# Coarser first weight loads, row tiles made ready in parts, and the first contexts evicted by one engine, in a fused normalise, attention and feed-forward kernel

## The chip, the cores and the metric

The kernel runs on one core of one Trainium2 chip. The metric is the device time of that core in microseconds (us), one number per execution. The time is the span of the profile plus about 1.8 us (924.28 and a span of 922.5 before the change), so differences of spans are differences of times.

## The reference, cut to what matters

```python
xn = _layernorm(A_x)                       # [2048, 640], bf16
# A: attention; 32 heads of 192, keys and values: the last 512 positions
q = (xn @ wq) ... ; p = softmax(q k^T * 192**-0.5); o = p v
s = o.reshape(2048, 32 * 192) @ wo
# B: feed-forward, F = 1536
g = silu((silu(xn @ w_gate) * (xn @ w_up)) @ w_down)
return A_x + s * g
```

The first 170 us or so are normalisation and feed-forward; the rest is attention, two heads (a pair) at a time, the 2048 rows in four blocks of 512.

## The kernel before

The **first loads** and the **head**: nothing can be multiplied before a row tile (128 rows) of x is loaded, normalised, transposed into `xnT` and its first weights are there. The four row tiles of block 0 are run one after the other through three hidden groups (`wg_sb` and `wu_sb`, 128 columns each), so that TensorE can start as soon as one row tile is ready.

```python
def load_x(t, eng=nc.sync):
    x_t[t] = lnx.tile([P, D], bf, name="x_t")
    if t == 0:
        for r, eng in ((lo, nc.sync), (hi, nc.scalar)):          # two halves, two queues
            eng.dma_start(out=x_t[t][r, :], in_=x2[t * P + r.start : t * P + r.stop, :])
    else:
        eng.dma_start(out=x_t[t][:], in_=x2[t * P : (t + 1) * P, :])
# ...
load_x(0)
load_x(1, nc.scalar)
for cs in (slice(0, 1), slice(1, 3), slice(3, NC)):              # 1, 2 and 2 of 5 chunks
    if cs.stop == NC:
        load_x(2)
    for eng, w_sb, w in ((nc.sync, wg_sb, B_w_gate), (nc.scalar, wu_sb, B_w_up)):
        src = w[cs.start * P : cs.stop * P, 0:FQ].rearrange("(c p) f -> p c f", p=P)
        eng.dma_start(out=w_sb[:, cs, 0:FQ], in_=src)
load_x(3)
# ... remaining weights, x tiles 4 to 7
nc.scalar.activation(act_t[:], one_t[:], ACT.Sqrt)               # table load
# ...
def ready(t):                       # transposes on TensorE, then a copy out of PSUM
    ln_transpose(t)
    n = NC if t else 2
    nc.scalar.copy(xnT[:, 0:n, rows], tps[t][:, 0:n, :])
    if n < NC:
        nc.vector.tensor_copy(out=xnT[:, n:NC, rows], in_=tps[t][:, n:NC, :])
# ...
for t in range(4):
    # order of the 30 matmuls of row tile t: chunk by chunk for t == 0
    for k, (f, s, cs) in enumerate(order):
        if k == len(order) * 3 // 5 and t < 3:
            ...                     # apply row tile t + 1, ready(t + 1)
        hidden_mm(first[f][s][:, rows], s, f, rows, cs)
```

The **normalisation of the next block** is spread over the hidden groups `f` of the current one, with a transposing DMA per row tile:

```python
if nx and 1 <= f < 5:
    ln_stats(4 * b + 3 + f)
    if f == 4:
        ln_rstd(b + 1, 0, 4)
if nx and 5 <= f < 9:
    ln_apply(4 * b + f - 1)
    ln_transpose_dma(4 * b + f - 1)
```

And the **attention part**: `q_rows` projects the queries in ten row-tiled matmuls and lets the held second half of an output projection in (`between`) before its last chunk; `divide` evicts a context (the product of probabilities and values) from PSUM. For the first two blocks of all, and for most of the last pair, the eviction was shared by VectorE and ScalarE:

```python
for c in range(NC):
    if c == NC - 1 and between:
        between()
    # two matmuls of chunk c
# ...
for k in range(2):
    if k == 0 and alone:            # VectorE, one instruction of 384 columns
        nc.vector.tensor_tensor(...)
        continue
    for h in range(2):              # ScalarE, two of 192 columns
        nc.scalar.activation(...)
```

The softmax here doesn't subtract the row's maximum and nothing guards it: scores larger than these inputs give would overflow.

Of the kernel before, what the change touches and what calls it, by code (L numbers as in the profile page):

```python
# [15 lines left out]
def kernel(  # L16
# [13 lines left out]
    nc = tc.nc  # L30
# [37 lines left out]
    qpool = ctx.enter_context(tc.tile_pool(name="att_q", bufs=2))  # L68
    psum = ctx.enter_context(tc.tile_pool(name="psum", bufs=2, space=bass.MemoryType.PSUM))

    def sc_tile():
        return psum.tile([P, 2, 512], f32, name="sc", tag="sc")

    def mm_tile():
        return psum.tile([P, 2, 512], f32, name="mm", tag="mm")

# [88 lines left out]
    with ExitStack() as fctx:  # L165
# [14 lines left out]
        def load_x(t, eng=nc.sync):  # L180
            x_t[t] = lnx.tile([P, D], bf, name="x_t")
            if t == 0:
                for r, eng in ((lo, nc.sync), (hi, nc.scalar)):
                    eng.dma_start(out=x_t[t][r, :], in_=x2[t * P + r.start : t * P + r.stop, :])
            else:
                eng.dma_start(out=x_t[t][:], in_=x2[t * P : (t + 1) * P, :])

# [8 lines left out]

        load_x(0)
        load_x(1, nc.scalar)
        for cs in (slice(0, 1), slice(1, 3), slice(3, NC)):
            if cs.stop == NC:  # L200
                load_x(2)
            for eng, w_sb, w in ((nc.sync, wg_sb, B_w_gate), (nc.scalar, wu_sb, B_w_up)):
                src = w[cs.start * P : cs.stop * P, 0:FQ].rearrange("(c p) f -> p c f", p=P)
                eng.dma_start(out=w_sb[:, cs, 0:FQ], in_=src)
        load_x(3)
        load_gu(1)
        for t in range(4, 8):
            load_x(t)
        load_gu(2)
        load_gu(3)  # L210
        nc.sync.dma_start(out=wd_sb[:], in_=B_w_down.rearrange("(f p) d -> p f d", p=P))


        nc.scalar.activation(act_t[:], one_t[:], ACT.Sqrt)
        warm = sc_tile()

        def keep_warm(n):
            for _ in range(n):
                nc.tensor.matmul(warm[:, 0, :], zero_t[:, 0:P], zero_t[:], start=True, stop=True)

        keep_warm(11)

# [34 lines left out]

        tps = {}

        def ln_transpose(t):  # L260
            xn = xns.pop(t)
            tps[t] = tp[:, t % 2, 0 : NC * P].rearrange("p (c k) -> p c k", c=NC)
            for c in range(NC):
                nc.tensor.transpose(tps[t][:, c, :], xn[:, c * P : (c + 1) * P], ident[:])

        def ln_transpose_dma(t):
# [18 lines left out]

        def ffn_hidden(b, f):
            gu = mm_tile() if (b, f) == (0, 3) else sc_tile()
            for s in range(2):
                hidden_mm(gu[:, s, :], s, f, slice(b * 512, (b + 1) * 512))
            hidden_gate(b, f, gu[:, 0, :], gu[:, 1, :])  # L290

# [26 lines left out]


        first = {f: [sc[:, s, :] for s in range(2)] for f, sc in ((0, sc_tile()), (1, sc_tile()))}  # L320
        tp = psum.tile([P, 2, 1024], bf, name="tp", tag="mm")
        first[2] = [mm[:, s, :] for mm in (mm_tile(),) for s in range(2)]
        def ready(t):
            ln_transpose(t)
            rows = slice(t * P, (t + 1) * P)
            n = NC if t else 2
            nc.scalar.copy(xnT[:, 0:n, rows], tps[t][:, 0:n, :])
            if n < NC:
                nc.vector.tensor_copy(out=xnT[:, n:NC, rows], in_=tps[t][:, n:NC, :])

        ln_stats(0)
        ln_sqrt(0)
        ln_stats(1, lambda: ln_apply(0, (slice(0, 2 * P), slice(2 * P, D))))
        ready(0)
        ln_sqrt(1)
        keep_warm(3)
        banks = [(f, s) for f in range(3) for s in range(2)]
        for t in range(4):
            rows = slice(t * P, (t + 1) * P)

            order = [(*fs, [c]) for c in range(NC) for fs in banks]
            if t:
                order = [(*fs, range(NC)) for fs in banks]
            for k, (f, s, cs) in enumerate(order):
                if k == len(order) * 3 // 5 and t < 3:
                    if t == 1:
                        ln_stats(3, lambda: ln_apply(2))
                    else:
                        ln_apply(t + 1)
                    ready(t + 1)  # L350
                    if t == 0:
                        ln_stats(2)
                    if t < 2:
                        ln_sqrt(t + 2)
                    else:
                        nc.scalar.activation(act_t[:], one_t[:], ACT.Silu)
                hidden_mm(first[f][s][:, rows], s, f, rows, cs)
                if t == 3 and s == 1:
                    hidden_gate(0, f, *first[f])
        nc.gpsimd.memset(V_p[:, :, :, Dh : Dh + 2], 1.0)  # L360

        for b in range(NB):
# [4 lines left out]
            for f in range(NF):  # L367
                if nx and b and f == 0:
                    for t in range(4 * b + 4, 4 * b + 8):
                        load_x(t)  # L370
                if b or f >= 3:
                    ffn_hidden(b, f)
                if nx and 1 <= f < 5:
                    ln_stats(4 * b + 3 + f)
                    if f == 4:
                        ln_rstd(b + 1, 0, 4)
                if nx and 5 <= f < 9:
                    ln_apply(4 * b + f - 1)
                    ln_transpose_dma(4 * b + f - 1)

# [40 lines left out]
    def q_rows(i, j, between=None):  # L421
# [4 lines left out]
        for c in range(NC):  # L426
            if c == NC - 1 and between:
                between()
            for h, r in enumerate((lo, hi)):
                nc.tensor.matmul(  # L430
                    q_ps[:, h, :], pairs[pr]["wq"][r, c, j * P : (j + 1) * P], xnT[r, c, b * 512 : (b + 1) * 512],
                    start=(c == 0), stop=(c == NC - 1),
                )
# [17 lines left out]
    def pv(i, q2):  # L451
# [4 lines left out]
        def part(p):  # L456
            if p == 0:
                if q2 == 0:
                    Obs[i] = opool.tile([P, 4, 2, Dh], bf, name="O_b")
                    tag = "OT_l" if late(i) and pr < last else "OT_b"  # L460
                    OTs[i] = otpool.tile([P, 12, P], bf, name=tag, tag=tag, bufs=2 if tag == "OT_l" else 3)
                st["alone"] = i < 2 or (pr == last and 2 * b + q2 < 5)
                st["acc"] = sc_tile() if st["alone"] and q2 and b < 2 else mm_tile()
            acc = st["acc"]
# [14 lines left out]
            if p == 3:  # L479
                divide(i, q2, acc, st["alone"])  # L480

        return [lambda p=p: part(p) for p in range(4)]

    def divide(i, q2, acc, alone):
        pr, b = divmod(i, NB)
# [4 lines left out]
        for k in range(2):  # L490
            qt = 2 * q2 + k
            a_k = a_v[:, k, :, :]
            if k == 0 and alone:
                nc.vector.tensor_tensor(
# [13 lines left out]
    def pv_full(i, q2):  # L508
# [6 lines left out]
        O_b, OT_b = Obs[i], OTs[i]  # L515
        alone = i < 2 or (pr == last and 2 * b + q2 < 5)
        acc = sc_tile() if alone and b == 1 else mm_tile()
        for k in range(2):
            qt = 2 * q2 + k
            for h in range(2):  # L520
                for kc in range(KC):
# [4 lines left out]
                    )  # L526
        divide(i, q2, acc, alone)

# [245 lines left out]
```

## Time and profile before

| | before |
|---|---|
| time, median of 3 runs | 924.18 us (924.05 to 924.45) |
| span of the profiled execution | 922.5 us |
| TensorE busy | 99% of the span |
| first real matmul | 6.88 us |
| row tiles 1, 2, 3 start | 9.79, 11.91, 14.02 us |
| first 512-column matmul ("end of the head") | 15.69 us |
| last group of matmuls | 918.04 us |

How to read it: with TensorE busy for 99% there are few places where time can be won: what lies before the end of the head, single stalls after it, and the tail behind the last matmul. Two distances will be used all along: the **end of the head**, where the first matmul of 512 columns starts, and the distance **from there to the last group of matmuls** (918.04 - 15.69 = 902.35 us before), which holds every stall that comes later.

### The profile page before, as it was taken

How to read it: one execution, taken by the hardware profiler on the slowest of the kernel's cores; microseconds unless marked ns; L12 is line 12 of the kernel's file. 1: busy time of each engine (PE TensorE's matmuls, PEld its weight loads, DVE VectorE, ACT ScalarE, POOL GpSimd, SP SyncE). 2: the span in 40 equal slices, each digit the busy share in tenths (PEclk: the TensorE clock that was granted, in tenths of full speed). 3: DMA queues.
4: the chain of work that ended last, by engine and by line, in shares of the span. 5: the costliest groups of instructions: out<-in, count | busy, mean ns of one | idle time of the engine just before them, and what ended most of it. 6: DMA issues, size and time to landing. Idle time of an engine off the chain costs nothing.

```text
span 922.5 us, 25778 instructions
## 1 busy us (share of the span) xinstructions
PE 915.9 (99%) x11085; PEld 624.4 (68%) x11101; DVE 575.7 (62%) x847; ACT 473.7 (51%) x847; POOL 101.6 (11%) x390
## 2 busy tenths in 40 slices
PE   9999999999999999999999999999999999999998
PEld 5455555575858586868686767676777777676666
DVE  6433331467676767676666667676767676767656
ACT  4222223556464656555556565655555555556561
POOL 0000000000000000000000000000000000002978
PEclk9999999999999999999999999999999999999999
DMA  9321510044544434444536262525271817163534
GB/s 293 78 53 35 114 35 1 1 74 93 88 78 83 83 79 88 72 93 65 102 57 109 55 112 53 113 45 121 41 125 36 131 37 123 32 124 92 120 71 141
DMA packets 243810, 77.18 MB, mean 84 GB/s; under 512 B 224624, under 2 KB 243696, under 8 KB 243696
## 3 DMA queue, kind: packets, MB, share of 16 engines
q1 hardware_dynamic: 242640, 74.73, 41.7%
q8 instruction: 87, 1.43, 0.7%
q10 hardware_dynamic: 1056, 0.80, 0.3%
q14 instruction: 27, 0.22, 0.1%
HBM read 39.45 MB, written 2.62 MB: 46 GB/s over the span
## 4 chain that ended last, share of the span: by engine, by line
PE 98%; DMA 1%; DVE 0%; ACTq 0%; issue 0%; POOLq 0%; POOL 0%; DVEq 0%
PE mm L430 22%; PE sc L567 19%; PE sc L444 18%; PE mm L470 16%; PE sc L276 11%; PE mm L298 6%; PE sc L539 3%; PE mm L522 2%; PE mm L539 1%; DMA wu_sb<-in_B_w_up_dram 1%; PE mm L276 0%; PE mm L311 0%; PE sc L470 0%; PE sc L522 0%; PE mm L444 0%
## 5 line engine op out<-in xcount | busy, mean ns | idle before, releaser
L448 ACT ACTIVATE p_t<-sc 128x1024 bf16<-128x1024 f32 x254 | 252.9, 1022 | 128.6 <-PE sc L444 128.6
L435 DVE TENSOR_REDUCE qT<-mm 128x512 bf16<-128x1024 f32 x189 | 231.0, 1223 | 92.5 <-PE mm L430 90.0
L500 ACT ACTIVATE O_b<-mm,r 128x192 bf16<-128x192 f32 x486 | 164.6, 421 | 183.4 <-issue 161.3
L430 PE MATMUL mm<-xnT,wq_p 64*128 64x512 bf16 x1890 | 240.1, 376 | 0.0
L592 DVE TENSOR_TENSOR sacc<-sacc,sc 128x640 f32<-128x640 f32 x200 | 164.3, 821 | 89.4 <-PE sc L567 89.4
L567 PE MATMUL sc<-wo_p,OT_b 64*128 64x320 bf16 x2592 | 217.2, 296 | 0.0
L444 PE MATMUL sc<-qT,khat 64*128 64x512 bf16 x1524 | 198.2, 376 | 0.1
L470 PE MATMUL mm<-V_p,p_t 64*128 64x193 bf16 x3520 | 186.3, 243 | 0.0
L470 PEld LDWEIGHTS <-p_t 64*128 64x128 bf16 x3584 | 162.6, 93 | 12.5 <-issue 0.4
L430 PEld LDWEIGHTS <-wq_p 64*128 64x128 bf16 x1890 | 105.2, 94 | 95.0 <-issue 0.5
L567 PEld LDWEIGHTS <-OT_b 64*128 64x128 bf16 x2592 | 140.1, 94 | 21.6
L444 PEld LDWEIGHTS <-khat 64*128 64x128 bf16 x1536 | 85.5, 94 | 79.4 <-issue 0.4
L555 POOL MEMSET turn_t<- 128x1 f32 x328 | 32.2, 98 | 696.4 <-PE mm L470 474.0
L284 DVE TENSOR_TENSOR hT<-sc,sg 128x512 bf16<-128x512 f32 x46 | 31.7, 690 | 85.2 <-ACT sg L283 85.1
L283 ACT ACTIVATE sg<-sc 128x512 bf16<-128x512 f32 x46 | 27.3, 596 | 72.4 <-PE sc L276 72.4
L276 PE MATMUL sc<-xnT,wu_sb 128*128 128x512 bf16 (+1 forms) x259 | 59.1, 355 | 0.3 <-DMA wu_sb<-in_B_w_up_dram 0.3
L276 PE MATMUL sc<-xnT,wg_sb 128*128 128x512 bf16 (+1 forms) x248 | 58.6, 354 | 0.6
L298 PE MATMUL mm<-wd_sb,hT 128*128 128x320 bf16 x384 | 56.6, 299 | 0.0
L489 DVE RECIPROCAL r<-mm 128x4 f32<-128x4 f32 x124 | 22.7, 183 | 47.4 <-PE mm L470 36.0
L298 PEld LDWEIGHTS <-hT 128*128 128x128 bf16 x384 | 37.5, 98 | 19.0
L276 PEld LDWEIGHTS <-wu_sb 128*128 128x128 bf16 x285 | 26.3, 98 | 27.2 <-DMA wu_sb<-in_B_w_up_dram 0.4
L276 PEld LDWEIGHTS <-wg_sb 128*128 128x128 bf16 x285 | 26.4, 98 | 23.2 <-DMA wg_sb<-in_B_w_gate_dram 0.2
(69 smaller groups left out, 373.8 us busy)
## 6 DMA issues: line engine op xcount, KB each, us to landing
wo_p<-in_A_wo_dram SPq DMA_DIRECT2D x16, 480.0 KB, 4.2
K_p<-in_A_k_cache_dram SPq DMA_DIRECT2D x32, 192.0 KB, 3.3
V_p<-in_A_v_cache_dram SPq DMA_DIRECT2D x32, 192.0 KB, 3.0
wq_p<-in_A_wq_dram SPq DMA_DIRECT2D x64, 80.0 KB, 3.1
wq_p<-in_A_wq_dram SPq DMA_DIRECT2D x16, 160.0 KB, 3.3
x_r<-in_A_x_dram SPq DMA_DIRECT2D x16, 160.0 KB, 4.1
x_t<-in_A_x_dram SPq DMA_DIRECT2D x14, 160.0 KB, 3.0
OT_b<-O_b SPq DMA_TRANSPOSE x124, 2.9
```

The lines of the kernel that those rows point to most:

```text
L276: nc.tensor.matmul(out, w_sb[:, c, f * P : (f + 1) * P], xnT[:, c, qc], start=(c == 0), stop=(c == NC - 1),)
L298: nc.tensor.matmul(dn[:, 0:HD], hTs[b][:, f, ti * P : (ti + 1) * P], wd_sb[:, f, cols], start=(f == 0), stop=(f == NF - 1),)
L430: nc.tensor.matmul(q_ps[:, h, :], pairs[pr]["wq"][r, c, j * P : (j + 1) * P], xnT[r, c, b * 512 : (b + 1) * 512], start=(c == 0), stop=(c ...
L435: nc.vector.reduce_sum(qTs[i][:, j, :], q_ps[:, :, :].rearrange("p h n -> p n h"), axis=AX.X)
L444: nc.tensor.matmul(sc[:, h, :], khat[r, j, ks], qT[r, j, :], start=(j == 0), stop=(j == 2))
L448: nc.scalar.activation(p_t[:, :, :], sc[:, :, :], ACT.Exp, scale=scale)
L470: m = nc.tensor.matmul(acc[:, k, h * 256 : h * 256 + Dh + 1], Ps[i][kc][r, h, qt * P : (qt + 1) * P], V_p[r, kc, h, 0 : Dh + 1], start=(p ...
L500: nc.scalar.activation(O_b[:, qt, h, :], a_k[:, h, 0:Dh], ACT.Copy, scale=r[:, k, h, :])
L539: nc.tensor.matmul(ps, OTs[i][:, 3 * qt + j, :], pairs[i // NB]["wo"][:, j, cols], start=(first and j == 0), stop=(end and j == 2),)
L555: st["turn"] = nc.gpsimd.memset(turn_t[:], 0.0)
L567: m = nc.tensor.matmul(ps[:, n, 0:HD], OTs[i][r, 3 * qt + j, :], pairs[i // NB]["wo"][r, j, n * HD : (n + 1) * HD], start=(turn == 0 and j ...
L592: nc.vector.tensor_tensor(s_t, s_t, sc[:, :, 0:HD], ALU.add)
```

## The change

Its intent: let row tile 0 start sooner and leave no hole behind it. x tiles 0 and 1 come whole on ScalarE's queue, the first quarter of the weights in two larger pieces (2 and 3 chunks of 5), all on SyncE's queue and ahead of x tiles 2 and 3. Row tile 0 is normalised, transposed and copied in three parts, the others in two. A context of the first two blocks is evicted by one engine; those of the last pair stay shared. Along with it went changes that the title does not name, among them other PSUM banks for the head, a shorter warm-up, an earlier table load, hidden group 3 of block 0 taken ahead of the loop over the hidden groups, the normalisation of the next block one hidden group later, and `between` one chunk earlier. The core of the diff:

```diff
-        load_x(0)
+        load_x(0, nc.scalar)
         load_x(1, nc.scalar)
-        for cs in (slice(0, 1), slice(1, 3), slice(3, NC)):
-            if cs.stop == NC:
-                load_x(2)
-            for eng, w_sb, w in ((nc.sync, wg_sb, B_w_gate), (nc.scalar, wu_sb, B_w_up)):
-                ...
+        load_first(slice(0, 2))        # wg then wu, both on SyncE's queue
+        load_first(slice(2, NC))
+        nc.scalar.activation(act_t[:], one_t[:], ACT.Sqrt)
+        load_x(2)
         load_x(3)
         load_gu(1)
+        load_gu(2)
         for t in range(4, 8):
             load_x(t)
-        load_gu(2)
 ...
-        keep_warm(11)
+        keep_warm(9)
+        keep_warm(6, P)
 ...
+        PARTS = {0: (slice(0, 1), slice(1, 3), slice(3, NC)), 1: (slice(0, 2), slice(2, NC))}
+        def ready(t, n):               # one part: its transposes, then its copy
 ...
-        ln_stats(1, lambda: ln_apply(0, (slice(0, 2 * P), slice(2 * P, D))))
-        ready(0)
+        ln_stats(1, lambda: ln_apply(0, COLS[0]))
+        for n in range(3):
+            ready(0, n)
         ln_sqrt(1)
-        keep_warm(3)
 ...
-                if k == len(order) * 3 // 5 and t < 3:
+                if t == 0 and k == 28:
+                    ln_apply(1, COLS[1])
+                    ready(1, 0)
+                elif t in (1, 2) and k == 24:
 ...
+        ffn_hidden(0, 3, ...)          # ahead of the loop
 ...
-                if b or f >= 3:
+                if b or f >= 4:
                     ffn_hidden(b, f)
-                if nx and 1 <= f < 5:
-                    ln_stats(4 * b + 3 + f)
-                    if f == 4:
+                if nx and 2 <= f < 6:
+                    ln_stats(4 * b + 2 + f)
+                    if f == 5:
                         ln_rstd(b + 1, 0, 4)
-                if nx and 5 <= f < 9:
+                if nx and 6 <= f < 10:
 ...
-            if c == NC - 1 and between:
+            if c == NC - 2 and between:
 ...
-                divide(i, q2, acc, st["alone"])
+                divide(i, q2, acc, (0, 1) if i < 2 and q2 == 0 else ())
```

## The prediction

> **What bounds the kernel now.** I read the page first (busy shares, then the chain that ended last), then the chain in order of time for the first 17 us, then the timeline of every engine from 0 to 16 us, then TensorE's timeline alone at the places of the attention part that the diff touches.
>
> From the page: the span, TensorE's busy row, its slices and the chain.
>
> ```profile
> span 922.5 us, 25778 instructions
> PE 915.9 (99%) x11085; PEld 624.4 (68%) x11101; DVE 575.7 (62%) x847; ACT 473.7 (51%) x847; POOL 101.6 (11%) x390
> ...
> PE   9999999999999999999999999999999999999998
> ...
> PE 98%; DMA 1%; DVE 0%; ACTq 0%; issue 0%; POOLq 0%; POOL 0%; DVEq 0%
> ```
>
> TensorE is the bound everywhere; only 6.6 us of the span are without a matmul. About 1.2 us are before the first one and about 4 us after the last (last matmul at 918.0 + 0.5 us). A busy row does not prove that matmuls run at full rate, so I checked start to start: in the attention part ten row-tiled matmuls of 512 columns start 1.08 us after the ten before them (0.216 us a pair), over whole stretches. What is left to win is therefore the head and single stalls. The head of the chain in order of time:
>
> ```profile
> 0.72 0.57 ACTq L184
> ...
> 1.95 0.45 ACTq L204
> ...
> 2.43 5.47 DMA wu_sb<-in_B_w_up_dram
> 7.90 0.05 issue
> 7.95 0.34 PE sc L276 x3
> ```
>
> The path runs through one weight transfer, the second wu piece (chunks 1 and 2), issued third on ScalarE's queue and landing at 7.90. The timeline around it:
>
> ```profile
> 3.66 0.89 DVE L229 BATCH_NORM_STATS2 stats<-x_t 128x6 f32<-128x320 bf16 x2 [2.49 <-DMA x_t<-in_A_x_dram]
> ...
> 5.36 0.64 DVE L253 TENSOR_SCALAR xn<-x_t,mv,rstd 128x256 bf16<-128x256 bf16 x2
> ...
> 6.43 0.37 ACT L327 COPY xnT<-tp 128x256 bf16<-128x256 bf16 x1 [1.30 <-PE tp L264]
> ...
> 6.88 0.22 PE L276 MATMUL sc<-xnT,wg_sb 128*128 128x128 bf16 x1
> ...
> 7.95 0.23 PE L276 MATMUL sc<-xnT,wu_sb 128*128 128x128 bf16 x1 [0.30 <-DMA wu_sb<-in_B_w_up_dram]
> ...
> 9.01 0.23 PE L276 MATMUL sc<-xnT,wg_sb 128*128 128x128 bf16 x1
> 9.02 0.10 PEld L276 LDWEIGHTS <-wu_sb 128*128 128x128 bf16 x1
> 9.05 0.69 ACT L327 COPY xnT<-tp 128x640 bf16<-128x640 bf16 x1 [2.05 <-PE tp L264]
> ...
> 10.17 0.45 DVE L253 TENSOR_SCALAR xn<-x_t,mv,rstd 128x640 bf16<-128x640 bf16 x1
> ```
>
> Row tile 0 gets its first real matmul at 6.88, loses about 0.5 us at 7.95 to the wu piece and a little at 9.01 to the last wg piece. Row tiles 1, 2 and 3 start at 9.79, 11.91 and 14.02. From 15.69 (the first 512-column matmul) nothing stalls in the hidden layer. Whatever is won at 15.69 is won at the end, since TensorE has no slack after it.
>
> **What the Trainium skill says.** "DMA: Bandwidth & Descriptors", section "Issuing engines are not separate DMA queues": transfers started by different engines run on the same 16 DMA engines and interleave; a second issuer only saves issue time. The trace agrees: between 7 and 12 us the DMA share is 1.01 to 1.10 at 328 to 367 GB/s with nearly all issues on SyncE, so moving the wu pieces from one queue to the other makes no bandwidth. "ScalarE: Activation LUTs", section "What ACT_TABLE_LOAD costs", gives 186 ns + 0.833 ns per column for an ACTIVATE with immediates. The copies here take 0.37 us for 256 columns and 0.69 for 640: the same slope, with a base of about 0.16. By the trace, 128 columns are then an estimated 0.26 us and 384 columns 0.48. "TensorE: Matmul & The Clock Gate", section "Part 1", says that the array runs at half clock until it has been busy about 3.4 us. Here the warm-up matmuls start 0.43 us apart until about 4.9 us and 0.22 later, so warm-up is still wanted and both kernels do some 4 us of it.
>
> **The change part by part.**
>
> (a) First loads. Now x tile 0 comes as two halves on two queues and the weights in 1, 2 and 2 chunks, gate on one queue and up on the other. After: x tiles 0 and 1 whole on ScalarE's queue; weights in 2 and 3 chunks, all four on SyncE's, before x tiles 2 and 3. The bytes needed until row tile 3 can start are the same (four x tiles of 160 KB and 960 KB of weights), but the order differs. By the stretch table, 0.52 MB were moved by 4.0 us, 0.94 by 6.0, 1.57 by 8.0, with a dip to 159 GB/s between 4 and 5. With the dip filled, at about 320 GB/s and with the 0.5 to 1.5 us between bytes moved and landing that the old pieces show, I estimate: x tile 0 at 3.9 (it was 3.5; it now shares the engines with the first gate piece), x tile 1 at 4.9 (was 4.1), first wg and wu 4.2 and 5.2, second wg 6.6, second wu 7.6, x tiles 2 and 3 at 8.2 and 8.8 (were 8.0 and 9.4). The Sqrt table load moves from 3.45 to about 1.95, but rstd ran at 4.85, right behind its statistics of 4.79: worth nothing.
>
> (b) Row tile 0 in three parts. Before, 1.52 us lie between the start of the first apply at 5.36 and the first matmul. After: 128 columns of apply, one transpose, a 0.26 us copy; but the transposes of part three stand before the first matmul and reuse the first PSUM bank, so they wait for copy one. Starting from apply at 5.66 (x tile 0 is 0.3 later): apply to 5.85, transpose to 6.15, copy to 6.41, two more transposes, first matmul 6.6, against 6.88. It runs 12 matmuls (0.67 us) to 7.27 and waits for the second wu piece at 7.6. The other 18 (1.0 us) follow with nothing to wait for.
>
> (c) Row tile 1 in two parts. Its transposes now stand 2 matmuls before the end of row tile 0 instead of 12. From the first transpose: 0.11 for two, about 0.2 to the copy, 0.37 copy, 0.05: 0.7 us, of which two matmuls and three transposes hide 0.3. Row tile 1 starts at about 9.2 (was 9.79). Tiles 2 and 3 have their transposes 6 matmuls before the end instead of 15. Row tile 2, however, hangs on xn of tile 2, and this on the chain x tile 2, statistics, Sqrt behind two copies on ScalarE (about 9.65), reciprocal, apply: done at about 10.65, as before (10.62). TensorE would wait some 0.15 us there; it then has 6 instead of 15 matmuls left and starts row tile 2 at 11.4 instead of 11.9, row tile 3 at about 13.6 instead of 14.02, with another 0.1 lost to the second copy. Net: about **0.3 us** won at 15.69.
>
> (d) Banks. Hidden group 3 writes the transpose banks instead of its own pair; these are free from about 14 us. The x tiles 4 to 7 come after the second quarter of weights; even then, at 0.32 MB per us, about 3.8 MB are through near 14 us, before VectorE wants them (17.8). Zero.
>
> (e) Contexts on one engine in the first two blocks. Now each is half VectorE (0.56 us), half ScalarE (two of 0.37), and ScalarE waits until VectorE's half is done. TensorE loses 0.11 at 195.49 and 0.13 at 199.36 to the ScalarE half. After, VectorE does all of the first (two of 0.48 start to start) and ScalarE all of the second (four, 1.43). Both losses go. But the second bank of block 1 comes free at about 200.45 and the output projection that reuses it wants it at 200.19: about 0.25 lost. Sum: **0.0**.
>
> (f) The held second half of the output projection moves one chunk (two matmuls, 0.22 us) earlier in the query projection. At one place it matters:
>
> ```profile
> 211.00 0.40 PE L430 MATMUL mm<-xnT,wq_p 64*128 64x512 bf16 x2
> 211.22 1.70 PE L444 MATMUL sc<-qT,khat 64*128 64x512 bf16 x12
> 211.22 0.82 DVE L590 COPY sacc<-sc 128x640 f32<-128x640 f32 x1 [0.85 <-PE sc L567]
> ```
>
> Twelve score matmuls take 1.52 us to the next start here and 1.30 elsewhere: the second six wait for the bank that VectorE empties until 212.04. Earlier by 0.22, it is free when wanted: **0.2 us** won. At the other 13 boundaries I looked at one (257.40): six scores, then ten projections, no stall, nothing to win.
>
> Sum: 0.3 + 0.0 + 0.2 = 0.5 us of 924.18: **923.7 us**.
>
> **The rivals.** First, *the loads set the head*: x tiles 0 and 1 land later than I think, since they share the engines with the weights that now go first; VectorE's order puts half of tile 1's statistics before tile 0's apply, so a late tile 1 holds tile 0 too. For it: x tile 0 has half the share it had. Against it: a stretch at 159 GB/s leaves room. It would eat the 0.3 and up to 0.3 more: 924.0 to 924.4. Second, *the parts work fully*: the two big pieces land by 7.2, and row tile 2's chain shifts with x tile 2; then row tiles 1 to 3 all keep 0.9 us: 923.0. Third, *the longer ScalarE eviction becomes a wait* beyond (e), 0.4 instead of 0.25, or the fewer matmuls behind the transposes expose each copy by 0.2: 924.0. Fourth, the clock drops in the pauses of 6 us after fewer warm-up matmuls; the old trace has pauses of 0.2 to 0.3 without a drop, so I give it little; it would cost 1 us or more.
>
> **Range and chances.** The parts are each uncertain by 0.3 to 0.5 us; together 0.7 either way: 922.9 to 924.5. All rivals lie within 0.2% of 924.18, and a change of 2% (18 us) would need TensorE idle in the attention part: 0.98 for same, 0.01 each for the others.
>
> **What would show it.** Right: first real matmul at 6.4 to 6.8; one wait for a wu piece at 7.3 to 7.6; row tile 1 starting 0.4 to 0.8 earlier, the first 512-column matmul near 15.4; no wait at the two places of (e) but a new one at the output projection near 200; twelve scores in 1.30 us near 211. Wrong: statistics of tile 1 waiting for its x tile, the first real matmul after 6.9, or row tile 2's transposes later than 10.7.

## The result, and the profile after

| | before | after |
|---|---|---|
| time, median of 6 runs each, same rounds | 924.16 us (923.96 to 924.82) | 923.33 us (923.02 to 924.13) |
| ratio | | 0.9991, 95% interval 0.9979 to 1.0004 |

A ratio is the mean time of one kernel's runs over the mean of the other's in the same rounds, so it is not quite the ratio of the medians in the table. The six times after are 923.98, 923.51, 923.10, 923.15, 924.13 and 923.02: four near 923.2 and two near 924.05. That split turned out to matter, because the profiled execution is the one of 923.98.

From the page of the changed kernel: the span, the busy row of the engines, and the chain that ended last by engine.

```profile
span 922.2 us, 25771 instructions
PE 914.6 (99%) x11086; PEld 626.9 (68%) x11102; DVE 576.3 (62%) x849; ACT 474.0 (51%) x851; POOL 101.5 (11%) x390
...
PE 98%; DMA 1%; issue 0%; SPq 0%; POOLq 0%; POOL 0%; DVE 0%; ACT 0%; DVEq 0%
```

Nothing has changed in kind: TensorE bounds the kernel, and what ends last starts from a DMA. The chain of waits in order of time (start, duration, what) names the same transfer as before, the second wu piece, now on SyncE's queue:

```profile
2.25 5.89 DMA wu_sb<-in_B_w_up_dram
8.13 0.05 issue
8.18 0.34 PE sc L276 x3
```

It used to land at 7.90 and now lands at 8.13. The timeline of the head, engine by engine (start, duration, engine, line, operation, result and inputs, shapes, and in brackets the idle time before it with its releaser):

```profile
3.78 0.89 DVE L237 BATCH_NORM_STATS2 stats<-x_t 128x6 f32<-128x320 bf16 x2 [2.60 <-DMA x_t<-in_A_x_dram]
...
6.54 0.22 PE L276 MATMUL sc<-xnT,wg_sb 128*128 128x128 bf16 x1
...
8.18 0.23 PE L276 MATMUL sc<-xnT,wu_sb 128*128 128x128 bf16 x1 [0.69 <-DMA wu_sb<-in_B_w_up_dram]
...
9.77 0.22 PE L276 MATMUL sc<-xnT,wg_sb 128*128 128x128 bf16 x1 [0.18 <-ACT xnT L332]
...
15.63 1.24 PE L276 MATMUL gu<-xnT,wg_sb 128*128 128x512 bf16 x4
```

The first real matmul comes at 6.54 instead of 6.88: the parts do that. Then TensorE stands still for 0.9 us, from its matmul at 7.26 to the next at 8.18, and row tile 1 starts at 9.77, as good as where it was (9.79). The end of the head moved by 0.06 us only. From there to the last group it is 917.96 - 15.63 = 902.33 us, against 902.35. So in this execution the change won next to nothing anywhere, as a sum, and yet four of the six runs were 0.8 us faster than this one. The attention part, where the prediction expected 0.2 us, first; the timeline around 211 us:

```profile
211.14 0.82 DVE L601 COPY sacc<-sc 128x640 f32<-128x640 f32 x1 [0.64 <-PE sc L578]
...
211.36 1.49 PE L456 MATMUL sc<-qT,khat 64*128 64x512 bf16 x12
...
212.67 1.26 PE L442 MATMUL mm<-xnT,wq_p 64*128 64x512 bf16 x10
```

The twelve scores take 211.36 to 212.67 = 1.31 us, not 1.52. So 0.21 us was won here and must have been lost elsewhere. The loss lies at the first hidden groups of block 1. Timeline of the changed kernel:

```profile
32.64 1.20 SPq L267 DMA_TRANSPOSE xnT<-xn  x1
...
33.97 1.24 PE L276 MATMUL sc<-xnT,wu_sb 128*128 128x512 bf16 x5
...
35.34 1.24 PE L276 MATMUL sc<-xnT,wg_sb 128*128 128x512 bf16 x5
```

and of the kernel before, the same two groups:

```profile
34.03 1.24 PE L276 MATMUL sc<-xnT,wu_sb 128*128 128x512 bf16 x5
...
35.11 1.24 PE L276 MATMUL sc<-xnT,wg_sb 128*128 128x512 bf16 x5
```

Every group of five of these stands 1.08 us after the last one; here it is 1.37 after the change, 0.29 more. The matmul that comes late is the first of block 1, which needs the last transposing DMA of block 1. That DMA is issued at 32.64 only and its last completion comes at 35.20 (33.71 before), because the normalisation of the next block was moved one hidden group later.

### The profile page after: what moved, and what is told of

It is laid out like the page before. It is cut to its first block, busy times and chain, and to the rows that moved or that the text cites. A ratio compares the mean times of both kernels' runs of the same rounds, so it can differ in the third digit from the quotient of the medians.

```text
span 922.2 us, 25771 instructions
## 1 busy us (share of the span) xinstructions
PE 914.6 (99%) x11086; PEld 626.9 (68%) x11102; DVE 576.3 (62%) x849; ACT 474.0 (51%) x851; POOL 101.5 (11%) x390
## 4 chain that ended last, share of the span: by engine, by line
PE 98%; DMA 1%; issue 0%; SPq 0%; POOLq 0%; POOL 0%; DVE 0%; ACT 0%; DVEq 0%
PE mm L442 22%; PE sc L578 19%; PE sc L456 18%; PE mm L481 16%; PE sc L276 11%; PE mm L298 6%; PE sc L550 3%; PE mm L533 2%; DMA wu_sb<-in_B_w_up_dram 1%; PE mm L550 1%; PE gu L276 0%; PE mm L311 0%; PE sc L533 0%; PE sc L481 0%; SPq L188 0%
```

## The experiments

Twelve kernels ran, five timed rounds each, all correct. Four sets shared chip and before runs: c1, d1, d2, d3 (before 924.41); h1 to h4 (before 924.42); q1, q2, v1 (before 924.30); q3 (before 924.46).

A trace is one execution: the head of the kernel before, unchanged in d1 and d2, ends at 15.69, 15.74 and 16.22 in three of them.

The theory after the result: the change wins in the head through the **order of the loads** first and the **parts** second, a late DMA can take it all back, and the normalisation one group later costs 0.3 us. Rivals: the gain comes from the parts alone; from the early table load; from the size of the pieces; or from the attention part, with the head only noise.

### c1: the changed kernel again

No edit. It asks whether the profiled execution was typical.

> The changed kernel unchanged, for its spread and a second trace of its head. Its six runs lie in two groups, 923.02 to 923.51 and 923.98 to 924.13, and the profiled one is in the upper. Theory (landing times): the groups differ by when the second wu piece lands (8.13 us in the profiled run), so a faster run shows it landing earlier and nothing else moved. Theory (a single wait elsewhere): the head is the same and the 0.28 us gap at the start of block 1 (35.05 to 35.34) is there in one group only. Time: median 923.2 to 923.7.

Measured: 923.23 us (922.98 to 923.51), ratio 0.9988 (0.9975 to 1.0000), before 924.41. Chain of waits, then timeline, of this execution:

```profile
2.25 5.13 DMA wu_sb<-in_B_w_up_dram
...
7.42 0.34 PE sc L276 x3
```

```profile
14.87 1.24 PE L276 MATMUL gu<-xnT,wg_sb 128*128 128x512 bf16 x4
```

The same transfer lands at 7.37 here, 0.76 us sooner than in the first profile, and the head ends at 14.87, also 0.76 sooner. The wait for it is 0.22 us beyond the normal spacing, and row tiles 1, 2 and 3 start at 9.01, 11.08 and 13.15. The gap at block 1 is there as well (33.21 to 34.58), so it is not what parts the two groups of runs. By their times, this is what most runs of the changed kernel look like; the profile taken first was one of its two late ones. Against the kernel before, c1's trace adds up as follows.

| part | how read | us |
|---|---|---|
| head | 14.87 - 15.69 | -0.82 |
| first groups of block 1 | 1.37 - 1.08 | +0.29 |
| contexts and the projection behind them | see d2 | -0.09 |
| twelve scores near 211 us | 1.31 - 1.52 | -0.21 |
| sum | | -0.83 |
| last group of matmuls | 917.23 - 918.04 | -0.81 |

All differences are accounted for to 0.02 us. The remaining part of the difference between the spans (922.5 to 921.5) lies in the tail: the last output transfer is issued 1.6 to 2.0 us after the last group and takes 2.5 to 2.9 us more, 4.2 to 4.5 together. Kernels built on the changed one lie at 4.22 to 4.44, those built on the one before at 4.42 to 4.53; whether 0.1 to 0.2 us of this belong to the change was not followed up.

### d1: the held projection one chunk earlier, alone

```diff
  (before)
-            if c == NC - 1 and between:
+            if c == NC - 2 and between:
```

> The kernel before with only the earlier drop of the held projection half. Theory: the twelve scores near 211 take 1.30 us instead of 1.52, and nothing else changes: 0.2 us faster, 923.9 to 924.0. Rival (a bound elsewhere takes the gain back): the local gap closes and the end does not move.

Measured: 924.18 us (923.78 to 924.36), against 924.41 before in the same rounds; ratio 0.9997 (0.9985 to 1.0010). The interval cannot tell 0.02% from nothing, but the trace can: the twelve scores take 211.27 to 212.58 = 1.31 us, and from the end of the head (15.74) to the last group (917.87) it is 902.13 us, 0.22 less than before. In the trace the 0.2 us are there, and they belong to this one line.

### d2: the contexts on one engine, alone

```diff
  (before)
-                st["alone"] = i < 2 or (pr == last and 2 * b + q2 < 5)
-                st["acc"] = sc_tile() if st["alone"] and q2 and b < 2 else mm_tile()
+                st["acc"] = sc_tile() if i < 2 and q2 else mm_tile()
 ...
-                divide(i, q2, acc, st["alone"])
+                divide(i, q2, acc, (0, 1) if i < 2 and q2 == 0 else ())
 ...
-            if k == 0 and alone:
+            if by_dve and k in by_dve:
```

> The kernel before with only the one-engine contexts of the first two blocks. Theory: the two losses at 195.49 (0.11 us) and 199.36 (0.13) go and a new one of some 0.15 to 0.25 at the first output projections of block 2 comes: between 0.1 us faster and 0.05 slower, 924.05 to 924.2. Rival (contexts are what made the change faster): 0.3 us or more faster.

Measured: 924.44 us (923.74 to 924.76), ratio 0.9999 (0.9985 to 1.0013). By its time nothing is to be seen (924.41 before), and it lies outside the expected range. From the end of the head (16.22 in this execution, one of its slower ones) to the last group (918.48) it is 902.26 us: 0.09 less than before. Where it comes from is seen best in the full change. TensorE's timeline before:

```profile
199.36 0.84 PE L470 MATMUL mm<-V_p,p_t 64*128 64x193 bf16 x16
200.02 0.99 PE L567 MATMUL sc<-wo_p,OT_b 64*128 64x320 bf16 x12
200.84 0.85 PE L470 MATMUL mm<-V_p,p_t 64*128 64x193 bf16 x16
```

and after, with ScalarE's eviction above it:

```profile
199.17 1.35 ACT L511 ACTIVATE O_b<-sc,r 128x192 bf16<-128x192 f32 x4 [2.40 <-DVE r L500]
...
200.01 1.15 PE L578 MATMUL sc<-wo_p,OT_b 64*128 64x320 bf16 x12
200.98 0.85 PE L481 MATMUL mm<-V_p,p_t 64*128 64x193 bf16 x16
```

The two old losses are gone: after the ten projections the contexts follow by 1.08 us (194.52 to 195.60) and not 1.19 (194.30 to 195.49), and the six output projections before 199.34 take 0.41 and not 0.54. In their place the first output projections of block 1 take 0.97 us (200.01 to 200.98) instead of 0.82, because the bank that ScalarE empties until 200.52 is wanted before. In sum -0.11 - 0.13 + 0.15 = -0.09.

### d3: the normalisation back to where it was

```diff
  (changed kernel)
-                if nx and 2 <= f < 6:
-                    ln_stats(4 * b + 2 + f)
-                    if f == 5:
+                if nx and 1 <= f < 5:
+                    ln_stats(4 * b + 3 + f)
+                    if f == 4:
 ...
-                if nx and 6 <= f < 10:
-                    ln_apply(4 * b + f - 2)
+                if nx and 5 <= f < 9:
+                    ln_apply(4 * b + f - 1)
```

> The changed kernel with the normalisation of the next block moved back to the hidden groups where it was before (statistics from group 1, apply and transpose from group 5). Theory (the last DMA transpose of block 1 lands at 35.2, just after TensorE wants it at 35.05): the gap of 0.28 us at 35.1 goes and the time falls by 0.28 against the changed kernel of the same chip, to 922.9 to 923.3. Rival (the gap is something else, for example a missing record or the clock): the gap stays and the time is that of the changed kernel.

Measured: 923.26 us (923.02 to 924.09), ratio 0.9989 (0.9977 to 1.0002), as good as c1. The gap at block 1 did go (33.44 to 34.52, 1.08), but one of the same size opened at hidden group 6:

```profile
20.21 1.24 PE L276 MATMUL sc<-xnT,wu_sb 128*128 128x512 bf16 x5
...
21.57 1.24 PE L276 MATMUL sc<-xnT,wg_sb 128*128 128x512 bf16 x5
```

1.36 instead of 1.08. On VectorE three statistics now stand ahead of the gate of group 4 (17.86 to 20.88), which in c1 starts at 20.01, so the PSUM bank of the group comes free late. In the kernel before, two stand ahead of a gate (17.80 to 19.83), because hidden group 3 is still inside the loop there. With group 3 taken ahead of the loop the old place has become too early for VectorE, and the new place is too late for the DMA: from the end of the head to the last group it is 917.16 - 14.81 = 902.35 us. The delay of the normalisation in the change was not a whim; but it traded one stall for another of the same size.

### h1 and h2: loads and parts apart

h1 is the changed kernel with the old first loads; h2 is the kernel before with the new ones.

```diff
  (h1: changed kernel)
-        load_x(0, nc.scalar)
+        load_x(0)                       # two halves, as before
         load_x(1, nc.scalar)
-        load_first(slice(0, 2))
-        load_first(slice(2, NC))
-        nc.scalar.activation(act_t[:], one_t[:], ACT.Sqrt)
-        load_x(2)
+        for cs in (slice(0, 1), slice(1, 3), slice(3, NC)):
+            ...                         # as before
```

```diff
  (h2: before)
-        load_x(0)
+        load_x(0, nc.scalar)            # whole
         load_x(1, nc.scalar)
-        for cs in (slice(0, 1), slice(1, 3), slice(3, NC)):
-            ...
+        load_first(slice(0, 2))
+        load_first(slice(2, NC))
+        nc.scalar.activation(act_t[:], one_t[:], ACT.Sqrt)
+        load_x(2)
```

> The changed kernel with the first loads of the kernel before (x tile 0 in halves on two queues, weights in 1, 2, 2 chunks on two queues, the Sqrt table load behind them, second and third weight quarters in the old order). Theory A (the loads win the head: with them the table load falls into a time when little is in flight, and no piece waits for an old transfer's semaphore): the first 512-column matmul is back at 15.4 to 15.8, the DMA rate dips again between 4 and 5.5 us, and the time is 924.0 to 924.3. Theory B (the parts of row tiles 0 and 1 win it, the loads are even): the first 512-column matmul at about 15.0 and 923.3 to 923.6.

> The kernel before with only the new first loads. Theory A: the first 512-column matmul near 15.1 to 15.3 (15.69 to 16.2 in the old one), no wait for a wg piece at 9.0, the DMA dip between 1.5 and 2.5 us, time 923.6 to 923.9 against some 924.3. Theory B: 924.2 to 924.5, the head unchanged but for the place of the wait.

Measured: h1 924.76 us (924.55 to 925.37), ratio 1.0006 (0.9993 to 1.0018), head 16.04. h2 923.96 us (923.69 to 924.09), ratio 0.9996 (0.9982 to 1.0009), head 15.06, and 902.34 us from there to the last group, as before.

In the traces, the new loads alone move the end of the head by 15.06 - 15.69 = -0.63 us; with the parts on top of them it is -0.82. The parts with the old loads (h1) end it at 16.04, +0.35 against the profile before, but within the 15.69 to 16.22 that the old head shows; by the times h1 is at +0.34, not clear of noise. So they win nothing there, and whether they lose is not shown. TensorE starts at 6.57 but runs out of weights three times, at 6.84, 7.25 and 8.51, since its small first piece is now used up sooner, and row tile 1's transposes wait behind all that. So the **loads carry the gain, and the parts pay only with them**. By the times it is -0.46 for h2, less than its trace says; its profiled execution was its fastest. Both point to theory A, but neither time is inside its range (924.0 to 924.3 for h1, 923.6 to 923.9 for h2).

The profiled execution of h1 was its slowest (925.37), and not for the head alone. It has a further 0.7 us that no other trace shows; TensorE's timeline:

```profile
203.16 0.58 PE L585 MATMUL sc<-wo_p,OT_b 64*128 64x320 bf16 x6 [0.56 <-DMA OT_b<-O_b]
```

A transposing DMA of a context came late there. Two of the five runs of h1 are some 0.6 us above the other three, which would fit; it was seen in one trace, and its cause stays open.

### h3: the table load first

Between 4 and 5 us the old loads have a dip. The changed kernel has none there, and by its table load at another time one could suspect that load. From the table by stretches (stretch, length, busy time and count of TensorE, its weight loads, VectorE, ScalarE and GpSimd, granted clock, DMA share, GB/s), the kernel before:

```profile
4.00:5.00 1.00, 1.00 (x4) 0.37 (x3) 0.97 (x4) 0.99 (x3) 0.00 (x0) 1.00 0.66 159
```

and c1:

```profile
4.00:5.00 1.00, 1.00 (x9) 0.54 (x7) 0.97 (x4) 0.12 (x1) 0.00 (x0) 1.00 1.07 341
```

ScalarE is loading its table (0.99 busy) in the one and not in the other. h3 puts the table load before everything:

```diff
  (changed kernel)
-        load_x(0, nc.scalar)
-        load_x(1, nc.scalar)
+        nc.scalar.activation(act_t[:], one_t[:], ACT.Sqrt)
+        load_x(0)
+        load_x(1)
         load_first(slice(0, 2))
         load_first(slice(2, NC))
-        nc.scalar.activation(act_t[:], one_t[:], ACT.Sqrt)
```

> The changed kernel with the Sqrt table load first on ScalarE (before any DMA moves) and the x tiles first on SyncE. If the table load is what holds the DMA (the dip moved with it from 4.0-5.5 to 1.5-2.5 us in six traces), the stretch from 2 to 3 us goes from 143-189 GB/s to 280 or more, the second wu piece lands 0.2 to 0.4 us earlier and the time is 0.1 to 0.4 under the changed kernel: 922.9 to 923.2. If the dip is only the start-up of the transfers, the rate from 2 to 3 us stays under 200 GB/s and the weights, now issued about 1 us later, land later: 923.3 to 923.8.

Measured: 924.06 us (923.92 to 924.71), ratio 0.9998 (0.9985 to 1.0010): worse than c1 and than both expectations. The table was loaded from 0.71 to 1.99. The stretch from 2 to 3 us did rise to 286 GB/s (189 in c1), as the suspicion had it, and yet there are dips later, with no table load near: 211 GB/s from 4 to 5, 242 from 7 to 8 and 264 from 8 to 9. The second wu piece landed at 8.15, its sixteen completions spread over 1.6 us, and the head ended at 15.64. Two runs made later settle it: q3 loads the table from 1.95 and dips to 145 GB/s from 4 to 5 all the same, and q1 loads it from 2.66 to 3.94 and moves 368 GB/s from 3 to 4. The suspicion against the table load falls for the dip from 4 to 5. What makes the dips **stays open**.

### h4: two row tiles of the next block at a time

d3 showed that the statistics must not come earlier and the last transposing DMA must. h4 keeps the late statistics and pairs the applications and transposes.

```diff
  (changed kernel)
-                if nx and 6 <= f < 10:
-                    ln_apply(4 * b + f - 2)
-                    ln_transpose_dma(4 * b + f - 2)
+                if nx and 6 <= f < 8:
+                    for t in (4 * b + 2 * f - 8, 4 * b + 2 * f - 7):
+                        ln_apply(t)
+                        ln_transpose_dma(t)
```

> The changed kernel with the statistics of the next block where the change has them, but its apply and DMA transpose two row tiles at a time (hidden groups 6 and 7 instead of 6 to 9). Moving all of it a group earlier closed the gap at block 1 but opened one as long (0.28 us) at hidden group 6, where three statistics stood before a gate on VectorE. If both gaps are as read, both are gone here and the time is 0.28 under the changed kernel: 922.8 to 923.1, with the first hidden matmul of block 1 1.08 us after the group before it. If not, another gap appears or the time stays at 923.2.

Measured: 923.06 us (runs 923.02, 922.74, 924.29, 924.23, 923.06), ratio 0.9990 (0.9978 to 1.0003). At block 1:

```profile
33.13 1.24 PE L276 MATMUL sc<-xnT,wu_sb 128*128 128x512 bf16 x5
...
34.21 1.24 PE L276 MATMUL sc<-xnT,wg_sb 128*128 128x512 bf16 x5
```

1.08 us, and hidden group 6 keeps its 1.08 too. From the end of the head (14.79) to the last group (916.83) it is 902.04 us: 0.32 less than c1's 902.36. The 0.29 of the late normalisation is thereby shown in the trace, and it is to be had back; the times, 923.06 and 923.23 from two chips, could not tell it. Two of its five runs belong to a late group again, near 924.25.

### q1, q2, q3: size of the pieces, or queue, or order

The trace keeps one completion record for each of the sixteen DMA engines that carry a transfer; a matmul may go only after the last. In us, for the second piece of each weight (second and third chunk before and in h1; third to fifth in the others):

| kernel | second wg: first, 15th, last | second wu: first, 15th, last |
|---|---|---|
| before | 4.64, 7.09, 7.38 | 5.64, 7.56, 7.90 |
| h1, old loads | 4.88, 6.87, 7.20 | 5.45, 7.41, 7.90 |
| after, profiled (late run) | 5.70, 6.17, 7.22 | 6.52, 7.01, 8.13 |
| c1, after again | 5.28, 6.08, 6.47 | 6.33, 6.97, 7.37 |
| h2, new loads | 5.38, 5.96, 6.00 | 6.30, 6.86, 6.89 |
| h4 | 5.46, 6.10, 6.14 | 6.43, 7.03, 7.12 |

With the old loads the sixteen come in over 2.3 to 2.7 us; with the new ones over 0.6 to 1.2 in the good runs. The late run of the changed kernel differs from c1 by **one** engine of sixteen: fifteen had delivered by 7.01, the last came 1.1 us later, and in each transfer after it one of the sixteen is as late. So this late run comes from a single late DMA engine. In q2's late run it is two; of the other late runs no trace was kept. Why an engine is late, no run here shows.

"DMA: Bandwidth & Descriptors", section "Why a DMA increments its semaphore by 16 and not by 1", in the Trainium skill says why this hurts: the engines of one transfer finish independently, and only the full 16 means that all data have landed. The table agrees, with 7.01 for fifteen and 8.13 for all.

Do the larger pieces cause the better landing, or that all is on one queue? q1 keeps the pieces and splits the queues; q2 keeps the queue and takes the old pieces.

```diff
  (q1: changed kernel)
-                nc.sync.dma_start(out=w_sb[:, cs, 0:FQ], in_=src)
+                (nc.sync if w_sb is wg_sb else nc.scalar).dma_start(out=w_sb[:, cs, 0:FQ], in_=src)
```

```diff
  (q2: changed kernel)
-        load_first(slice(0, 2))
-        load_first(slice(2, NC))
+        for cs in (slice(0, 1), slice(1, 3), slice(3, NC)):
+            load_first(cs)
```

> The changed kernel with the two early wu pieces on ScalarE's queue behind the x tiles; piece sizes as in the change; the table load thereby back at about 2.6 us. In the traces with the old loads the sixteen completions of one transfer lie 2 us and more apart from the second weight pieces on (4.64 to 7.38), with the new ones 0.6 to 1.2. Theory P (spreading the weights over two queues lets the DMA engines drift apart): the spread is over 1.5 us again, the first 512-column matmul is at 15.4 or later, time 923.9 to 924.4. Theory Q (pieces and their count decide): spread under 1.2 us, head at 14.8 to 15.0, 923.0 to 923.5.

> The changed kernel with the early weights in 1, 2 and 2 chunks, six transfers, all on SyncE as in the change. Theory Q (large pieces matter, by fewer transfers and fewer waits for an old transfer's semaphore): x tiles 2 and 3 are issued 1 us later and land later, head at 15.2 or later, 923.6 to 924.0. Theory P (the single queue matters, not the size): head within 0.2 us of the change's 14.8 to 14.9, 923.0 to 923.5.

Measured: q1 924.22 us (924.13 to 924.35), ratio 0.9999 (0.9987 to 1.0012). q2 923.36 us (runs 924.10, 923.11, 923.36, 923.27, 923.69), ratio 0.9991 (0.9979 to 1.0004); its profiled execution was the late one (head 15.72), with two engines late, so no trace shows the head of its usual run. TensorE in q1:

```profile
8.21 0.23 PE L276 MATMUL sc<-xnT,wu_sb 128*128 128x128 bf16 x1 [0.86 <-DMA wu_sb<-in_B_w_up_dram]
```

By the times the size of the pieces does not matter: q2 in its usual run is as fast as c1. The queue does. All five runs of q1 are above 924.1, and its head ends at 15.65, 0.78 us later than c1's (a stray 0.3 us of the profiled execution lies elsewhere, at 531 us). But my explanation for it was only half right: I had expected the completions to spread as widely as with the old loads, and those of the second wu piece span 1.0 us (7.19 to 8.16). They are late as a whole: half of them have come at 7.49. Issued at 2.14, 0.11 us earlier than in c1, the piece lands 0.79 us later. Meanwhile x tiles 2 and 3, which no one needs yet, have moved up on the other queue: tile 2 is issued at 1.74 and lands at 6.52, tile 3 is issued at 2.26, behind the piece, and has half of its completions at 7.21 (the expectation of q3 below calls it tile 2). "Queues, rings and completion order" in the same page says that each DMA engine takes turns between the queue rows, packet by packet. The order of the piece and tile 3 agrees with that: what stands on the other queue takes its share although it is needed later. How much of the 0.79 us comes from tile 2 going out first, and how much from the sharing, these runs do not part.

q3 asks the reverse, whether one queue is enough. It is the kernel before with its wu pieces on SyncE's queue, in their old order.

```diff
  (before)
-            for eng, w_sb, w in ((nc.sync, wg_sb, B_w_gate), (nc.scalar, wu_sb, B_w_up)):
+            for eng, w_sb, w in ((nc.sync, wg_sb, B_w_gate), (nc.sync, wu_sb, B_w_up)):
```

> The kernel before with nothing changed but the queue of the three early wu pieces: SyncE's, alternating with the wg pieces, instead of ScalarE's. Pieces of 1, 2 and 2 chunks, the halves of x tile 0, the place of x tile 2 and the waits for old transfers' semaphores stay. With the weights on two queues the second wu piece landed after x tile 2, which was issued behind it (8.16 against 7.86 us); on one queue before it. Theory (a needed transfer shares the 16 DMA engines with whatever the other queue holds behind it; on one queue it is served in order): the second wu piece lands at 7.0 or earlier (7.4 to 8.4 in the old traces), the first 512-column matmul at 15.0 to 15.3, time 923.7 to 924.0, as with the new loads. Rival (the semaphore waits and the placing of the table load were what cost): the head stays at 15.6 or later and the time at 924.2 to 924.5.

Measured: 924.38 us (924.24 to 924.71), ratio 1.0000 (0.9986 to 1.0014). The second wu piece did land early, at 6.60, but head (15.82) and time came out as the rival had them. TensorE waited for the third pieces instead:

```profile
8.75 0.23 PE L276 MATMUL sc<-xnT,wg_sb 128*128 128x128 bf16 x1 [0.35 <-DMA wg_sb<-in_B_w_gate_dram]
...
9.27 0.23 PE L276 MATMUL sc<-xnT,wu_sb 128*128 128x128 bf16 x1 [0.29 <-DMA wu_sb<-in_B_w_up_dram]
```

These were issued at 4.22 and 4.70, behind x tile 2. The rival's reasons do not fit: the issues follow each other without a pause for an old semaphore, and the table load moved up to 1.95. In the kernel before, too, the third wg piece goes out at 3.58 only. In the changed kernel the last weight that row tile 0 needs is issued at 2.25 us. So what helps is not one thing: in the kernels whose head ends early, the weights that are needed first are **issued from the start, on one queue, in the order of need, ahead of the x tiles that can wait**, and x tiles 0 and 1 go out beside them on the other queue. One queue and this order are not enough by themselves: h3 has both, with x tiles 0 and 1 ahead on the same queue, issues its second wu piece at 3.13, and its head ends at 15.64; in its trace twelve engines had delivered that piece by 7.01 and four came up to 1.1 us later. Why they are late in h3, whose five runs all lie above 923.9, stays open.

### v1: a shorter chain on VectorE

With h4's repair and no late engine, the head waits for VectorE, which works from 3.6 to past 10 us and pauses only for ScalarE's square roots. v1 shortens what stands there: row tile 0 is applied in one instruction, the square root of row tile 1 goes ahead of the third copy, and row tile 1's transposes move up.

```diff
  (changed kernel, with h4's edit)
-        ln_stats(1, lambda: ln_apply(0, COLS[0]))
+        ln_stats(1, lambda: ln_apply(0))
         for n in range(3):
             ready(0, n)
-        ln_sqrt(1)
+            if n == 1:
+                ln_sqrt(1)
 ...
-                if t == 0 and k == 28:
+                if t == 0 and k == 20:
                     ln_apply(1, COLS[1])
                     ready(1, 0)
+                elif t == 0 and k == 25:
+                    ready(1, 1)
 ...
             if t == 0:
-                ready(1, 1)
                 ln_stats(2)
```

> The kernel with the next block's apply two tiles at a time, and besides: row tile 0 applied in one piece (0.45 us instead of 0.83) but still transposed and copied in three, its rstd for row tile 1 ahead of the last copy on ScalarE, and row tile 1's transposes at matmuls 20 and 25 instead of 28 and 30. Theory (where no DMA engine is late, VectorE's chain over tiles 0, 1 and 2 bounds the head: it has hardly an idle moment from 3.75 to 10.2): the first matmul 0.1 later, row tile 1 at 8.5 instead of 8.8, the first 512-column matmul at 14.5 instead of 14.8, time 0.2 to 0.3 under the variant without it, 922.6 to 922.9. Rival (the weights bound it also then): the same head, 923.0 to 923.1.

Measured: 922.76 us (922.47 to 922.96), ratio 0.9983 (0.9970 to 0.9997); before 924.30.

```profile
14.59 1.24 PE L276 MATMUL gu<-xnT,wg_sb 128*128 128x512 bf16 x4
```

The head ends 0.20 us sooner than that of h4 (14.79), on which v1 is built, and 0.28 sooner than c1's, although its first real matmul is later than in either (6.58 against 6.51 and 6.47). Row tile 1 starts at 8.72 (h4: 8.81), row tile 2 at 10.80 (11.00). Applying row tile 0 in one instruction of 0.45 us instead of three of 0.83 together frees VectorE for row tiles 1 and 2; that this is what won, and not the other two edits, no run parts. (Its first four matmuls stand 0.10 us apart and not 0.055, like the 128-column warm-up matmuls before them; why was not followed up.) From there to the last group it is 902.08 us. It is the fastest kernel and the only one whose interval leaves out 1. None of its five runs was late; five runs are too few to say that it cannot be. It ran in no common round with the changed kernel; against their own before runs v1 is at -1.54 us and c1 at -1.18.

## Why the prediction was right or wrong

The prediction was right in its time (923.7 against 923.33, in the range of 922.9 to 924.5). Its sum of 0.5 us was short by 0.3, and it came that close by luck: two errors of opposite sign met, +0.52 in the head and -0.29 at block 1.

- **What bounds the kernel.** Right, but for a slip: the second wu piece is the fourth transfer on ScalarE's queue and not the third. What was won at the end of the head was won at the end, in every trace, but for the stalls listed.
- **(a) First loads.** The order of events was right, and the dip between 4 and 5 us was filled. Of the landings it foresaw, x tile 0 was said to come at 3.9 and was used from 3.78, the second wu piece at 7.6 and came at 7.37 (c1) or 8.13 (the late run). It said that moving a piece to another queue "makes no bandwidth", which h2 and q1 do not contradict; but it booked the gain under the parts, (b) and (c), and not under the loads. Its landing times hold it already: row tile 0's last weights come at 7.6 in them and came at 8.97 before.
- **(b) Row tile 0 in three parts.** Right: first real matmul foreseen at 6.6, measured 6.54 and 6.47; the wait for the second wu piece foreseen at about 7.3 to 7.6, measured at 7.14 to 7.42 in c1. But h1 shows that the parts win nothing with the old loads.
- **(c) The other row tiles.** This term was mis-sized. Row tile 1 was to start at 9.2 (c1: 9.01), row tile 2 at 11.4 (11.08), row tile 3 at 13.6 (13.15). The prediction held row tile 2 to its old time of 10.65 by the chain on VectorE, with the Sqrt behind two copies on ScalarE at 9.65. In c1 x tile 2 landed at 7.82 (estimated 8.2), VectorE began on it at 8.02, as early as before (8.08), and the two copies, now of row tile 1's parts, ran from 8.58; so the Sqrt came at 9.23, the apply ended at 10.21, and TensorE reached row tile 2's transposes at 10.34 and did not wait. The head gained 0.82 us and not 0.3.
- **(d) Banks, "Zero".** This step failed. It looked at the loads of x tiles 4 to 7 only and passed over the three lines of the diff that move the normalisation one hidden group later. They cost 0.29 us, at the first matmul of block 1 (c1, undone by h4).
- **(e) Contexts, "0.0".** Right in mechanism: both losses gone, a new wait at the output projection near 200 us. The new wait was put at 0.25 and is 0.15, so the sum is -0.09.
- **(f) The held projection, 0.2.** Right: 0.21 in c1, and d1 has it alone.
- **Rivals.** "The parts work fully" (923.0) is what most runs show, though for the loads' sake rather than the parts'; "the loads set the head" (924.0 to 924.4) has the time of the late runs, but not their mechanism: in the one profiled, x tiles 0 and 1 landed at 3.75 and 4.71, sooner than foreseen, and the second wu piece was late. The prediction named both and saw one time between them; the kernel does now this, now that. Row tile 0's later VectorE chain did not bite, and the clock did not drop: in the changed kernel the matmuls of 128 columns stay 0.055 us apart.

Put together, for a usual run: 0.82 (head) - 0.29 + 0.09 + 0.21 = 0.83 us won; for a late one, 0.06 - 0.29 + 0.09 + 0.21 = 0.07. Four of the first six runs were of the one kind and two of the other.

What stays open: why single DMA engines are late in some runs, and several in h3, what makes the dips in the DMA rate, and why h1 lost 0.7 us to one transposing DMA.

## What to carry to other kernels

At the start of a kernel, issue the bytes that the first matmuls need in the order of need, ahead of everything that can wait, and try which queue carries what: here the first weights on one queue and the first x tiles on the other won, while weights on both (q1) or everything on one (h3) did not; work cut into finer parts pays only when its data are there. When an early stage gets faster or moves, look again at what was timed to it: here the next block's normalisation fitted neither its old place nor its new one, and pairing it won 0.3 us back. And before explaining one profile, see where its run lies among the others: this one was a late run, and its trace alone would have taught that the change does nothing. Differences of 0.1%, as here, are seen in traces and hardly in times.

## What the Trainium skill lacked or had wrong

- "DMA: Bandwidth & Descriptors", section "Issuing engines are not separate DMA queues", says that a second issuer saves issue time only. It lacks that it can cost: with the first wu pieces on ScalarE's queue the kernel took 924.22 us (q1), with all on SyncE's 923.36 (q2, same rounds, smaller pieces). In q1 x tile 2, which could wait, landed at 6.52 and the second wu piece, which could not, at 8.16.
- The same page, section "Why a DMA increments its semaphore by 16 and not by 1", gives no figure for how far apart the completions of one transfer lie. Here, for the second pieces of the weights, it was 0.5 us at best (second wu piece of d3, 6.56 to 7.07), 2.8 at worst (that of d2, 5.59 to 8.43), and once a single engine was 1.1 us behind the other fifteen (after, 7.01 and 8.13). I found no page that has an engine fall behind for a whole stretch in one execution and not in the next.
- "ScalarE: Activation LUTs", section "What ACT_TABLE_LOAD costs", adds about 1.38 us of drain to a load of about 1.28. The load agrees (1.28 us at 3.45 in the kernel before), but no drain shows in this place: the next ACTIVATE starts at 4.74, 0.01 us after the load's end. Nor does it at the second load (13.98 to 15.26): the copy before it ends at 13.96 and the ACTIVATE after it starts at 15.28.
